# An attention kernel followed by a two-layer block: weights in larger packets, loads reordered, layer work moved forward, decay rows copied directly, the M banks handed out from one tile

## Chip, cores and metric

One core of a Trainium2 chip. The time is device time of the whole program in microseconds. The fast runs of one kernel lie within 1.7% of each other here, most within 1%; ratios below are computed between runs of the same rounds on the same chip. One run of all, at a granted clock of 0.56 against 0.97 to 0.99 in the others, is called slow and left out of the ratios. In the lines of the profile PE is TensorE, PEld its weight loads, DVE VectorE, ACT ScalarE, POOL GpSimd, SP SyncE, and L367 is line 367 of the kernel.

## The reference, cut to what matters

Eight batches of eight heads, 576 positions, head size 64. Causal attention with a decay bias from a running sum of `s`, then a two-layer block over all 4,608 rows.

```python
scores = q @ k.T / sqrt(64)
cum = cumsum(maximum(s, 0))
bias = -(cum[:, None] - cum[None, :])            # clipped at 0, causal mask
attn = softmax(scores + bias) @ v                # x: 4608 x 512
h = x @ w_in                                     # 512 x 2048
out = (h * clip(h + 3, 0, 6) / 6) @ w_out        # 2048 x 512
```

## The kernel before

Heads go in 32 pairs. A pair's q and k are loaded (256-byte rows), cast to f16 on GpSimd, transposed on TensorE; the decay is added through extra rows of kT and qT ("decay rows"). The block runs in nine blocks of 512 rows; a "layer task" is four 512-column matmuls. The kernel uses eight PSUM banks: two called M, three S, two O, one Y. The parts that matter:

```python
cpool / work / psum pools ...
w_in_sb = cpool.tile([128, KC, DFF], F16, tag="c_win")
...
def banks(early):                      # transposes of the first pairs borrow M
    return dict(tag="M", bufs=2) if early else dict(tag="S", bufs=3)
...
def load_w_in(c):                      # four loads, 512 columns each
    nc.gpsimd.dma_start(out=w_in_sb[:, :, c * 512:(c + 1) * 512],
        in_=moe_w_in[:, c * 512:(c + 1) * 512].rearrange("(kc p) f -> p kc f", p=128))
...
def m1(n, f):                          # layer 1
    ph = psum.tile([128, 512], F32, tag="M", bufs=2)      # a new tile for each task
    for kc in range(KC):
        nc.tensor.matmul(out=ph, lhsT=w_in_sb[:, kc, f * 128:(f + 1) * 128],
                         rhs=xT[:, kc, n * 512:(n + 1) * 512], ...)
    trl = work.tile([128, 512], F32, tag="trl", bufs=3)
    nc.scalar.activation(out=trl, in_=ph, func=AF.Relu, bias=bias3[:, 0:1], scale=1.0)
    nc.vector.scalar_tensor_tensor(out=gT[n][:, f, :], in0=trl, scalar=6.0, in1=ph, ...)

def m2(n, t4, part):                   # layer 2; four parts make one output
    if part == 0:
        pouts[n, t4] = psum.tile([128, 512], F32, tag="Y", bufs=1)
...
load_qk(0, nc.sync); load_v(0, nc.scalar); load_qk(1, nc.sync); load_v(1, nc.sync)
load_qk(2, nc.sync); load_v(2, nc.sync)
...                                    # decay rows: SBUF -> DRAM -> rows of each pair
weave(att_of[1], m1_tasks(0))
for n in range(NBLK - 1):
    att = att_of[n + 2] if n + 2 < B else []
    weave(att, merged(m1_tasks(n + 1), m2_tasks(n)))
```

The order of instructions on each engine is the order of this code; the semaphore waits between engines are put in by the framework.

The softmax here doesn't subtract the row's maximum and nothing guards it: scores larger than these inputs give would overflow.

Of the kernel before, what the change touches and what calls it, by code (L numbers as in the profile page):

```python
# [16 lines left out]
def kernel(  # L17
# [23 lines left out]
    GRAN = 10  # L41
    VW = D + 2
# [6 lines left out]
    psum = ctx.enter_context(tc.tile_pool(name="psum", bufs=1, space=bass.MemoryType.PSUM))  # L49

# [68 lines left out]

    def load_qk(p, eng):  # L120
        b, h0 = (2 * p) // H, (2 * p) % H
        t = work.tile([128, NTR, 2, D], F32, tag="qkf", bufs=3, name=f"qkf{p}")
        for i, src in enumerate((q, k)):
            eng.dma_start(
                out=t[:, :, i, :],
                in_=src[b, h0:h0 + 2].rearrange("h s d -> (h s) d").rearrange(
                    "(t p) d -> p t d", p=128
                ),
            )
        qk_f[p] = t  # L130
# [20 lines left out]
    def cast_qk(p):  # L151
        t = work.tile([128, NTR, 2, D], F16, tag="qkh", bufs=2)
        nc.gpsimd.tensor_copy(out=t, in_=qk_f.pop(p))  # L153
        qk_h[p] = t

    def cast_v(p):
        sl = p % NS
        eng = nc.vector if p in (1, 2, 3, 4) else nc.gpsimd
        eng.tensor_copy(out=v_h[:, sl, :, :, 0:D], in_=v_f[:, sl])  # L159

    def banks(early):

        return dict(tag="M", bufs=2) if early else dict(tag="S", bufs=3)

    def transpose_group(p, g):
        t0, t1 = ((0, 5), (5, 9))[g]
        n = (t1 - t0) * 128
        pT = psum.tile([128, 640], F16, **banks(p < 5))
        src = qk_h[p]
        for t in range(t0, t1):  # L170
            nc.tensor.matmul(  # L171
                out=pT[:, (t - t0) * 128:(t - t0 + 1) * 128],
                lhsT=src[:, t, :, :],
                rhs=ident,
                is_transpose=True,
                start=(t == t0),
                stop=(t == t1 - 1),
            )
        sl = p % NS
        c0 = t0 * 128  # L180
        nc.vector.tensor_copy(out=qT[0:64, sl, c0:c0 + n], in_=pT[0:64, 0:n])  # L181
        nc.vector.tensor_copy(out=kT[0:64, sl, c0:c0 + n], in_=pT[64:128, 0:n])  # L182
        if g == 1:
            qk_h.pop(p)
# [95 lines left out]
    def x_transpose(p):  # L280
        b, hp = p // (H // 2), p % (H // 2)
        xs = x_tiles.pop(p)
        pX = psum.tile([128, 640], F16, **banks(p < 3))
# [12 lines left out]
    def load_w_in(c):  # L296
        nc.gpsimd.dma_start(
            out=w_in_sb[:, :, c * 512:(c + 1) * 512],
            in_=moe_w_in[:, c * 512:(c + 1) * 512].rearrange("(kc p) f -> p kc f", p=128),
        )  # L300

    def load_w_out(c):
        nc.gpsimd.dma_start(
            out=w_out_sb[:, c * 4:(c + 1) * 4, :],
            in_=moe_w_out[c * 512:(c + 1) * 512, :].rearrange("(ft p) j -> p ft j", p=128),
        )

# [4 lines left out]
    def m1(n, f):  # L312
        if f == 0:
            gT[n] = work.tile([128, NF, 512], F16, tag="gT", bufs=2, name=f"gT{n}")
        ph = psum.tile([128, 512], F32, tag="M", bufs=2)
        for kc in range(KC):
            nc.tensor.matmul(  # L317
                out=ph,
                lhsT=w_in_sb[:, kc, f * 128:(f + 1) * 128],
# [10 lines left out]
    def m2(n, t4, part):  # L330
        if part == 0:
            pouts[n, t4] = psum.tile([128, 512], F32, tag="Y", bufs=1, name=f"po{n}_{t4}")
# [17 lines left out]


    load_qk(0, nc.sync)
    load_v(0, nc.scalar)
    load_qk(1, nc.sync)
    load_v(1, nc.sync)
    load_qk(2, nc.sync)
    load_v(2, nc.sync)
    mask_rows(0, nc.scalar.copy)
    nc.scalar.activation(out=qaug, in_=c8, func=AF.Copy, scale=-1.0)
    mask_rows(1, nc.scalar.copy)  # L360
    nc.scalar.dma_start(
        out=kaug_dram.rearrange("r (h t) -> h r t", h=NH), in_=kaug
    )
    nc.scalar.dma_start(out=qaug_dram.rearrange("r (h t) -> h (r t)", h=NH), in_=qaug)
    load_aug(0, nc.scalar)
    load_aug(1, nc.scalar)


    def keep_warm(n):
        pw = psum.tile([128, 512], F32, tag="M", bufs=2, name="pw")  # L370
# [5 lines left out]
    weights = {  # L376
        1: [(load_w_in, 0)],
# [128 lines left out]
```

## Time and profile before

| | before |
|---|---|
| median, range | 399.7 us, 396.7 to 401.4 (3 runs) |
| span of the profiled run | 397.3 us |
| TensorE busy | 366.4 us (92%), idle almost only in the first 80 us and at the end |
| DMA engines | full for the first 80 us, half busy to about 280 us, then a tenth or so |

The lines themselves are in the prediction. Read them so: where the row of TensorE is all nines at full clock, only less work on TensorE can save time; where it is not, ask what the chain of waits names.

### The profile page before, as it was taken

What the parts mean: (1) busy time and instruction counts of PE and PEld (TensorE: products, weight loads), DVE (VectorE), ACT (ScalarE), POOL (GpSimd) and SP (SyncE); (2) the same over time, 40 slices, a digit from 0 to 9 for tenths busy, and PEclk for the clock granted to TensorE, in tenths of its full rate; (3) what the DMA queues carried; (4) which work ended last, traced back from release to release, by engine and by line L of the source; (5) the groups of instructions that cost most, each with busy time, mean ns of one, the idle gap of its engine ahead of it and who ended that gap; (6) DMA issues with size and microseconds to landing.
All of it is one profiled execution on the core that took longest, in us unless ns stands there. A gap on an engine that the chain in (4) does not pass through costs nothing.

```text
span 397.3 us, 8194 instructions
## 1 busy us (share of the span) xinstructions
PE 366.4 (92%) x3040; PEld 209.7 (53%) x3040; DVE 227.2 (57%) x417; ACT 210.8 (53%) x406; POOL 140.3 (35%) x333
## 2 busy tenths in 40 slices
PE   7584776899999999999999999999999999999985
PEld 3363443555555555555555555555555544444432
DVE  4574372756666666666666666666665564454511
ACT  6364473755555566666666555555556633443400
POOL 3394825544444444444444444444443200000000
PEclk9999698999999999999999999999999999999999
DMA  9999999955555555554555455455100001010111
GB/s 176 201 213 205 185 208 178 194 108 118 116 118 118 119 117 118 119 117 117 118 118 118 108 126 114 109 126 116 38 28 27 28 26 54 26 53 28 49 58 54
DMA packets 123512, 43.40 MB, mean 109 GB/s; under 512 B 114192, under 2 KB 118672, under 8 KB 123472
## 3 DMA queue, kind: packets, MB, share of 16 engines
q1 hardware_dynamic: 117456, 37.89, 43.9%
q0 software_dynamic: 4224, 4.19, 6.4%
q10 hardware_dynamic: 1792, 0.79, 0.9%
q8 instruction: 24, 0.39, 0.4%
q14 instruction: 16, 0.13, 0.1%
HBM read 37.32 MB, written 9.73 MB: 118 GB/s over the span
## 4 chain that ended last, share of the span: by engine, by line
PE 80%; DMA 10%; POOL 4%; DVE 3%; ACT 2%; issue 1%; SPq 0%; POOLq 0%; ACTq 0%
PE po L335 31%; PE ph L317 29%; PE S L211 8%; DMA qkf<-in_k_dram 7%; PE O L260 6%; PE pT L171 3%; PE pX L285 2%; POOL Pm L224 2%; POOL t L153 1%; DMA kaug_scratch<-kaug 1%; DMA kT<-kaug_scratch 1%; ACT trl L325 1%; ACT Pm L219 1%; DMA s_sb<-in_s_dram 1%; DVE osb L344 1%; DVE gT L326 1%
## 5 line engine op out<-in xcount | busy, mean ns | idle before, releaser
L326 DVE SCALAR_TENSOR_TENSOR gT<-trl,ph 128x512 f16<-128x512 f32 x144 | 98.8, 687 | 114.7 <-ACT trl L325 114.5
L219 ACT ACTIVATE Pm<-S 128x384 f16<-128x384 f32 (+2 forms) x256 | 113.7, 506 | 80.3 <-PE S L211 72.5
L317 PE MATMUL ph<-xT,w_in_sb 128*128 128x512 f16 x576 | 147.4, 381 | 0.0
L335 PE MATMUL po<-w_out_sb,gT 128*128 128x512 f16 x576 | 144.4, 379 | 2.3 <-DVE osb L344 2.3
L325 ACT ACTIVATE trl<-ph,bias 128x512 f32<-128x512 f32 x144 | 99.6, 692 | 82.8 <-PE ph L317 81.0
L224 POOL TENSOR_SCALAR_AFFINE_SELECT Pm<-Pm 128x128 f16<-128x128 f16 (+2 forms) x256 | 78.8, 313 | 154.6 <-ACT Pm L219 144.8
L211 PE MATMUL S<-qT,kT 128*128 128x320 f16 (+4 forms) x448 | 71.4, 265 | 8.0 <-DMA kT<-kaug_scratch 3.0
L335 PEld LDWEIGHTS <-gT 128*128 128x128 f16 x576 | 51.2, 98 | 49.4 <-issue 3.2
L317 PEld LDWEIGHTS <-w_in_sb 128*128 128x128 f16 x576 | 52.2, 98 | 44.5 <-issue 1.1
L211 PEld LDWEIGHTS <-kT 128*128 128x128 f16 x448 | 42.1, 99 | 35.3 <-issue 4.9
L153 POOL CAST t<-qkf 128x1152 f16<-128x1152 f32 x32 | 36.7, 1147 | 21.4 <-DMA qkf<-in_k_dram 21.4
L260 PEld LDWEIGHTS <-Pm 128*128 128x128 f16 x960 | 37.4, 97 | 7.8 <-POOL Pm L224 1.6
L260 PE MATMUL O<-v_h,Pm 128*128 128x65 f16 x960 | 40.8, 193 | 0.5 <-POOL Pm L224 0.5
L171 PE MATMUL pT<-ident,t 128*128 128x128 f16 x288 | 26.8, 222 | 13.5 <-POOL t L153 12.9
L181 DVE COPY qT<-pT 64x640 f16<-64x640 f16 x64 | 28.3, 442 | 17.7 <-PE pT L171 17.6
L171 PEld LDWEIGHTS <-t 128*128 128x128 f16 x288 | 21.1, 99 | 28.1 <-POOL t L153 14.6
L344 DVE TENSOR_SCALAR osb<-po 128x512 f32<-128x512 f32 x36 | 24.8, 690 | 13.8 <-PE po L335 13.2
L182 DVE COPY kT<-pT 64x640 f16<-64x640 f16 x64 | 29.4, 459 | 0.9
L272 DVE TENSOR_TENSOR xs<-O,r 128x640 f16<-128x640 f32 x32 | 26.4, 824 | 1.1
L159 POOL CAST v_h<-v_f 128x640 f16<-128x640 f32 x28 | 20.1, 718 | 0.0
L285 PEld LDWEIGHTS <-xs 128*128 128x128 f16 x160 | 11.8, 99 | 10.9 <-issue 6.2
L293 DVE COPY xT<-pX 128x576 f16<-128x576 f16 x32 | 14.5, 453 | 1.7 <-PE pX L285 1.5
(29 smaller groups left out, 56.6 us busy)
## 6 DMA issues: line engine op xcount, KB each, us to landing
qkf<-in_q_dram SPq DMA_DIRECT2D x32, 288.0 KB
qkf<-in_k_dram SPq DMA_DIRECT2D x32, 288.0 KB
out_dram<-osb SPq DMA_DIRECT2D x36, 256.0 KB
v_f<-in_v_dram SPq DMA_DIRECT2D x62, 128.0 KB
w_in_sb<-in_moe_w_in_dram POOLq DMA_DIRECT2D x4, 512.0 KB, 8.1
w_out_sb<-in_moe_w_out_dram POOLq DMA_DIRECT2D x4, 512.0 KB, 10.1
v_f<-in_v_dram SPq DMA_DIRECT2D x31, 32.0 KB
kT<-kaug_scratch SPq DMA_DIRECT2D x30, 6.8 KB
```

What stands on the lines that cost most here:

```text
L153: nc.gpsimd.tensor_copy(out=t, in_=qk_f.pop(p))
L171: nc.tensor.matmul(out=pT[:, (t - t0) * 128:(t - t0 + 1) * 128], lhsT=src[:, t, :, :], rhs=ident, is_transpose=True, start=(t == t0), stop ...
L182: nc.vector.tensor_copy(out=kT[0:64, sl, c0:c0 + n], in_=pT[64:128, 0:n])
L211: nc.tensor.matmul(out=S[:, c:c + hi - lo], lhsT=kT[:, sl, off + 128 * kt:off + 128 * (kt + 1)], rhs=qT[:, sl, off + lo:off + hi], start=( ...
L219: nc.scalar.activation(out=P[:, p0:p0 + n], in_=S[:, 0:n], func=AF.Exp, scale=0.125, bias=0.0)
L224: nc.gpsimd.affine_select(out=view, in_=view, pattern=pattern, compare_op=ALU.is_ge, fill=0.0, base=0, channel_multiplier=-1,)
L260: nc.tensor.matmul(out=O[:, hh, qt * VW:qt * VW + D + 1], lhsT=P[:, c:c + 128], rhs=v_h[:, sl, hh, kt, 0:D + 1], start=(qt == 0), stop=(qt ...
L317: nc.tensor.matmul(out=ph, lhsT=w_in_sb[:, kc, f * 128:(f + 1) * 128], rhs=xT[:, kc, n * 512:(n + 1) * 512], start=(kc == 0), stop=(kc == ...
L325: nc.scalar.activation(out=trl, in_=ph, func=AF.Relu, bias=bias3[:, 0:1], scale=1.0)
L326: nc.vector.scalar_tensor_tensor(out=gT[n][:, f, :], in0=trl, scalar=6.0, in1=ph, op0=ALU.min, op1=ALU.mult)
L335: nc.tensor.matmul(out=po, lhsT=gT[n][:, f, t4 * 128:(t4 + 1) * 128], rhs=w_out_sb[:, f, :], start=(f == 0), stop=(f == NF - 1),)
L344: nc.vector.tensor_scalar_mul(out=osb, in0=po, scalar1=1.0 / 6.0)
```

## The change

Its intent: weights in 4 and 8 KB packets, loads in order of need, one and a half layers of block 0 beside batch 1, decay rows of pair 0 from SBUF to SBUF. The diff, cut to its core:

```diff
+    Mt = psum.tile([128, 2, 512], F32, tag="M", bufs=1)      # both M banks
+    ring = [0]
+    def bank():
+        ring[0] ^= 1
+        return Mt[:, ring[0], :]
 ...
-        ph = psum.tile([128, 512], F32, tag="M", bufs=2)
+        ph = bank()                       # also early transposes, warm-up
 ...
-                lhsT=w_in_sb[:, kc, f * 128:(f + 1) * 128],
+                lhsT=w_in_t[:, kc, f // 8, f % 8, :],        # every eighth column
 ...
-    def load_w_in(c):                     # 4 loads of 512 columns
+    def load_w_in(h):                     # 2 loads of 1024 columns
+            in_=moe_w_in[:, h * 1024:(h + 1) * 1024]...
+            in_=moe_w_out[h * 1024:(h + 1) * 1024, :].rearrange("(p f) j -> p f j", f=8)[:, f0:f0 + 4, :]
 ...
+            if (n, t4) in ((0, 1), (8, 1), (8, 3)):
+                pouts[n, t4] = bank()
 ...
-    load_v(0, nc.scalar)                  # and v 1, qk 2, v 2 at once on SyncE
+    for hh in range(2):                   # decay rows of pair 0, SBUF to SBUF
+        nc.sync.dma_start(out=kT[64:65, 0, c0:c1], in_=kaug[hh:hh + 1, 0, :])
+        nc.scalar.dma_start(out=qT[67:68, 0, c0:c1], in_=qaug[hh:hh + 1, :])
+    ...
+    load_v(0, nc.sync)                    # then kaug, qaug to DRAM, v 1, qk 2 ...
 ...
+    weights_at = {1: [(load_w_in, 0)], 2: [(load_w_in, 1)]}
+    pairs_at = {0: [3], 1: [4], 2: [], 3: [5], 4: [6], 5: [7, 8]}
 ...
+    first = [(task, 0.0 if f < 4 else 0.7) for f, (task, _) in enumerate(m1_tasks(0))]
+    for c, f in enumerate((0, 2, 5, 8)):  # w_out loads ride on layer tasks
+    weave(att_of[1], first + m2_0[:8])
+    weave(att_of[2], merged(m1_tasks(1), m2_0[8:], 2))
```

A branch for loads by partition is in the new source too, but its switch is 0 and it is never taken.

More of the change, by code (lines that the diff above doesn't have):

```diff
@@ L41 @@
     GRAN = 10
+    PTN = 0
     VW = D + 2
@@ L118, with by_partition @@
     qk_h = {}
+    def by_partition(p):
+        return p < PTN
     def load_qk(p, eng):
         b, h0 = (2 * p) // H, (2 * p) % H
-        t = work.tile([128, NTR, 2, D], F32, tag="qkf", bufs=3, name=f"qkf{p}")
+        t = work.tile([128, NTR * 2 * D], F32, tag="qkf", bufs=3, name=f"qkf{p}")
         for i, src in enumerate((q, k)):
-            eng.dma_start(
-                out=t[:, :, i, :],
-                in_=src[b, h0:h0 + 2].rearrange("h s d -> (h s) d").rearrange(
-                    "(t p) d -> p t d", p=128
-                ),
-            )
+            rows = src[b, h0:h0 + 2].rearrange("h s d -> (h s) d")
+            if by_partition(p):
+                eng.dma_start(
+                    out=t.rearrange("p (i t d) -> p i t d", i=2, d=D)[:, i],
+                    in_=rows.rearrange("(p t) d -> p t d", t=NTR),
+                )
+            else:
+                eng.dma_start(
+                    out=t.rearrange("p (t i d) -> p t i d", i=2, d=D)[:, :, i, :],
+                    in_=rows.rearrange("(t p) d -> p t d", p=128),
+                )
         qk_f[p] = t
@@ L152, in cast_qk @@
         t = work.tile([128, NTR, 2, D], F16, tag="qkh", bufs=2)
-        nc.gpsimd.tensor_copy(out=t, in_=qk_f.pop(p))
+        f = qk_f.pop(p)
+        if by_partition(p):
+            nc.gpsimd.tensor_copy(
+                out=t.rearrange("p t i d -> p i t d"),
+                in_=f.rearrange("p (i t d) -> p i t d", i=2, d=D),
+            )
+        else:
+            nc.gpsimd.tensor_copy(
+                out=t, in_=f.rearrange("p (t i d) -> p t i d", i=2, d=D)
+            )
         qk_h[p] = t
@@ L157, in cast_v, with half_bank, transpose_tile @@
         sl = p % NS
-        eng = nc.vector if p in (1, 2, 3, 4) else nc.gpsimd
-        eng.tensor_copy(out=v_h[:, sl, :, :, 0:D], in_=v_f[:, sl])
-    def banks(early):
-        return dict(tag="M", bufs=2) if early else dict(tag="S", bufs=3)
+        copy = nc.vector.tensor_copy if p in (1, 2, 3, 4) else nc.gpsimd.tensor_copy
+        copy(out=v_h[:, sl, :, :, 0:D], in_=v_f[:, sl])
+    def half_bank(early):
+        if early:
+            return bank().bitcast(F16)[:, 0:640]
+        return psum.tile([128, 640], F16, tag="S", bufs=3, name="pT")
+    def transpose_tile(out, src, first, last):
+        nc.tensor.matmul(
+            out=out, lhsT=src, rhs=ident, is_transpose=True, start=first, stop=last
+        )
     def transpose_group(p, g):
@@ L167, in transpose_group, with transpose_pair @@
         n = (t1 - t0) * 128
-        pT = psum.tile([128, 640], F16, **banks(p < 5))
+        pT = half_bank(p < 5)
         src = qk_h[p]
         for t in range(t0, t1):
-            nc.tensor.matmul(
-                out=pT[:, (t - t0) * 128:(t - t0 + 1) * 128],
-                lhsT=src[:, t, :, :],
-                rhs=ident,
-                is_transpose=True,
-                start=(t == t0),
-                stop=(t == t1 - 1),
+            c = (t - t0) * 128
+            transpose_tile(pT[:, c:c + 128], src[:, t, :, :], t == t0, t == t1 - 1)
+        sl = p % NS
+        c0 = t0 * 128
+        for dst, r0 in ((qT, 0), (kT, 64)):
+            nc.vector.tensor_copy(out=dst[0:64, sl, c0:c0 + n], in_=pT[r0:r0 + 64, 0:n])
+        if g == 1:
+            qk_h.pop(p)
+    def transpose_pair(p):
+        pT = Mt.rearrange("p a b -> p (a b)").bitcast(F16)[:, 0:W2]
+        src = qk_h.pop(p)
+        for t in range(NTR):
+            transpose_tile(
+                pT[:, t * 128:(t + 1) * 128], src[:, t, :, :], t in (0, 8), t in (7, 8)
             )
         sl = p % NS
-        c0 = t0 * 128
-        nc.vector.tensor_copy(out=qT[0:64, sl, c0:c0 + n], in_=pT[0:64, 0:n])
-        nc.vector.tensor_copy(out=kT[0:64, sl, c0:c0 + n], in_=pT[64:128, 0:n])
-        if g == 1:
-            qk_h.pop(p)
+        for dst, r0 in ((qT, 0), (kT, 64)):
+            nc.vector.tensor_copy(
+                out=dst[0:64, sl, 0:W2].rearrange("d (p t) -> d p t", t=NTR),
+                in_=pT[r0:r0 + 64].rearrange("d (t p) -> d p t", p=128),
+            )
     BANKS = [
@@ L282, in x_transpose @@
         xs = x_tiles.pop(p)
-        pX = psum.tile([128, 640], F16, **banks(p < 3))
+        pX = half_bank(p < 3)
         for qt in range(5):
@@ L293, in x_transpose @@
         nc.vector.tensor_copy(out=xT[:, hp, b * SEQ:(b + 1) * SEQ], in_=pX[:, 0:SEQ])
-    def load_w_in(c):
+    def load_w_in(h):
         nc.gpsimd.dma_start(
-            out=w_in_sb[:, :, c * 512:(c + 1) * 512],
-            in_=moe_w_in[:, c * 512:(c + 1) * 512].rearrange("(kc p) f -> p kc f", p=128),
+            out=w_in_sb[:, :, h * 1024:(h + 1) * 1024],
+            in_=moe_w_in[:, h * 1024:(h + 1) * 1024].rearrange("(kc p) f -> p kc f", p=128),
         )
     def load_w_out(c):
+        h, f0 = c // 2, (c % 2) * 4
         nc.gpsimd.dma_start(
             out=w_out_sb[:, c * 4:(c + 1) * 4, :],
-            in_=moe_w_out[c * 512:(c + 1) * 512, :].rearrange("(ft p) j -> p ft j", p=128),
+            in_=moe_w_out[h * 1024:(h + 1) * 1024, :].rearrange("(p f) j -> p f j", f=8)[
+                :, f0:f0 + 4, :
+            ],
         )
+    w_in_t = w_in_sb.rearrange("p k (h m f) -> p k h f m", h=2, f=8)
     gT = {}
@@ L331, in m2 @@
         if part == 0:
-            pouts[n, t4] = psum.tile([128, 512], F32, tag="Y", bufs=1, name=f"po{n}_{t4}")
+            if (n, t4) in ((0, 1), (8, 1), (8, 3)):
+                pouts[n, t4] = bank()
+            else:
+                pouts[n, t4] = psum.tile([128, 512], F32, tag="Y", name=f"po{n}_{t4}")
         po = pouts[n, t4]
@@ L349 @@
     nc.vector.memset(bias3, 3.0)
-    load_qk(0, nc.sync)
-    load_v(0, nc.scalar)
-    load_qk(1, nc.sync)
-    load_v(1, nc.sync)
-    load_qk(2, nc.sync)
-    load_v(2, nc.sync)
-    mask_rows(0, nc.scalar.copy)
-    nc.scalar.activation(out=qaug, in_=c8, func=AF.Copy, scale=-1.0)
-    mask_rows(1, nc.scalar.copy)
-    nc.scalar.dma_start(
-        out=kaug_dram.rearrange("r (h t) -> h r t", h=NH), in_=kaug
-    )
-    nc.scalar.dma_start(out=qaug_dram.rearrange("r (h t) -> h (r t)", h=NH), in_=qaug)
-    load_aug(0, nc.scalar)
-    load_aug(1, nc.scalar)
     def keep_warm(n):
-        pw = psum.tile([128, 512], F32, tag="M", bufs=2, name="pw")
+        pw = bank()
         for i in range(n):
@@ L374, in keep_warm @@
             )
-    weights = {
-        1: [(load_w_in, 0)],
-        2: [(load_w_in, 1), (load_w_in, 2)],
-        3: [(load_w_in, 3)],
-        4: [(load_w_out, 0), (load_w_out, 1)],
-        5: [(load_w_out, 2), (load_w_out, 3)],
-    }
+    load_qk(0, nc.sync)
+    load_qk(1, nc.sync)
+    mask_rows(0, nc.scalar.copy)
+    nc.scalar.activation(out=qaug, in_=c8, func=AF.Copy, scale=-1.0)
+    for hh in range(2):
+        c0, c1 = hh * SEQ, (hh + 1) * SEQ
+        nc.sync.dma_start(out=kT[64:65, 0, c0:c1], in_=kaug[hh:hh + 1, 0, :])
+        nc.scalar.dma_start(out=qT[67:68, 0, c0:c1], in_=qaug[hh:hh + 1, :])
+    for hh in range(2):
+        c0, c1 = hh * SEQ, (hh + 1) * SEQ
+        nc.sync.dma_start(out=kT[65:66, 0, c0:c1], in_=kaug[hh:hh + 1, 1, :])
+        nc.scalar.dma_start(out=kT[66:67, 0, c0:c1], in_=kaug[hh:hh + 1, 2, :])
+    load_v(0, nc.sync)
+    nc.sync.dma_start(
+        out=kaug_dram.rearrange("r (h t) -> h r t", h=NH), in_=kaug
+    )
+    nc.sync.dma_start(out=qaug_dram.rearrange("r (h t) -> h (r t)", h=NH), in_=qaug)
+    mask_rows(1, nc.scalar.copy)
+    load_v(1, nc.sync)
+    load_qk(2, nc.sync)
+    load_aug(1, nc.sync)
+    load_v(2, nc.sync)
+    weights_at = {1: [(load_w_in, 0)], 2: [(load_w_in, 1)]}
+    pairs_at = {0: [3], 1: [4], 2: [], 3: [5], 4: [6], 5: [7, 8]}
     def att_tasks(p):
+        more = p + 1 < NP
         def loads():
@@ L389, in loads @@
                 load_aug(p + 2, nc.sync)
-            if p + 3 < NP:
-                load_qk(p + 3, nc.sync)
-                load_v(p + 3, nc.sync)
-            for load, c in weights.get(p, []):
-                load(c)
-        more = p + 1 < NP
-        tasks = [(loads, 0)]
-        for bi in range(4):
-            tasks.append((lambda bi=bi: scores_bank(2 * p, bi), 400))
-        if p > 0:
-            tasks.append((lambda: attend(2 * p - 1), 1200))
-        if more:
-            tasks.append((lambda: transpose_group(p + 1, 0), 640))
-        for bi in range(4):
-            tasks.append((lambda bi=bi: scores_bank(2 * p + 1, bi), 400))
+            for m in pairs_at.get(p, [p + 3] if p + 3 < NP else []):
+                load_qk(m, nc.sync)
+                load_v(m, nc.sync)
+            if p > 4 and more:
+                cast_qk(p + 1)
         def casts():
@@ L409, in casts, with scores @@
                 cast_v(p + 1)
-            if p + 2 < NP:
+            if p + 2 <= 4:
                 cast_qk(p + 2)
-        tasks.append((casts, 0))
-        if p > 0:
-            tasks.append((lambda: x_transpose(p - 1), 640))
-        if more:
-            tasks.append((lambda: transpose_group(p + 1, 1), 512))
-        tasks.append((lambda: attend(2 * p), 1200))
-        return tasks
+            for load, c in weights_at.get(p, []):
+                load(c)
+        def scores(hd):
+            return [(lambda bi=bi: scores_bank(hd, bi), 400) for bi in range(4)]
+        if not more:
+            tr = []
+        elif by_partition(p + 1):
+            tr = [[(lambda: transpose_pair(p + 1), 1152)], []]
+        else:
+            tr = [[(lambda: transpose_group(p + 1, 0), 640)],
+                  [(lambda: transpose_group(p + 1, 1), 512)]]
+        here = tr if p != 4 else []
+        a = [(loads, 0)] + scores(2 * p)
+        a += here[0] if here else []
+        a += [(lambda: attend(2 * p - 1), 1200)] if p > 0 else []
+        a += scores(2 * p + 1) + [(casts, 0)]
+        a += here[1] if here else []
+        a += [(lambda: x_transpose(p - 1), 640)] if p > 0 else []
+        c = [(lambda: attend(2 * p), 1200)]
+        if p == 4:
+            c += [(lambda: cast_qk(p + 1), 0)] + tr[0] + tr[1]
+        return a, c
+    att_of = [[]]
+    for p in range(NP):
+        a, c = att_tasks(p)
+        att_of[-1] += a
+        if p % 4 == 0 and p > 0:
+            att_of.append([])
+        att_of[-1] += c
+    att_of[-1] += [(lambda: attend(NH - 1), 1200), (lambda: x_transpose(NP - 1), 640)]
     def weave(att, mlp):
         total = float(sum(c for _, c in att)) or 1.0
-        done = 0.0
-        for i, task in enumerate(mlp):
-            while att and done / total < i / len(mlp):
+        whole = float(sum(w for _, w in mlp))
+        done, due = 0.0, 0.0
+        for task, w in mlp:
+            while att and done / total < due / whole:
                 a, c = att.pop(0)
@@ L430, in weave @@
             task()
+            due += w
         for a, c in att:
@@ L434, in m1_tasks, with merged @@
     def m1_tasks(n):
-        return [lambda f=f: m1(n, f) for f in range(NF)]
+        return [(lambda f=f: m1(n, f), 1.0) for f in range(NF)]
     def m2_tasks(n):
-        return [lambda t4=t4, part=part: m2(n, t4, part) for t4 in range(4) for part in range(4)]
-    def merged(a, b):
-        out_ = []
-        for t in range(4):
-            f, g = a[4 * t:4 * t + 4], b[4 * t:4 * t + 4]
-            out_ += [g[0], g[1], f[0], g[2], f[1], g[3], f[2], f[3]]
+        return [
+            (lambda t4=t4, part=part: m2(n, t4, part), 1.0)
+            for t4 in range(4) for part in range(4)
+        ]
+    def merged(a, b, rounds):
+        out_ = []
+        na = len(a) // rounds
+        for t in range(rounds):
+            f, g = a[na * t:na * (t + 1)], b[4 * t:4 * t + 4]
+            if na == 4:
+                out_ += [g[0], g[1], f[0], g[2], f[1], g[3], f[2], f[3]]
+            else:
+                out_ += [g[0], f[0], f[1], g[1], f[2], f[3], g[2], f[4], g[3]] + f[5:]
         return out_
-    keep_warm(22)
+    keep_warm(18)
     cast_qk(0)
-    transpose_group(0, 0)
-    transpose_group(0, 1)
+    if by_partition(0):
+        transpose_pair(0)
+    else:
+        transpose_group(0, 0)
+        transpose_group(0, 1)
     mask_rows(2, nc.vector.tensor_copy)
@@ L454 @@
     cast_qk(1)
-    keep_warm(10)
-    att_all = []
-    cut = []
-    for b in range(B):
-        for p in range(4 * b, 4 * b + 4):
-            att_all += att_tasks(p)
-            if p % 4 == 0:
-                cut.append(len(att_all) - 2)
-    att_all += [(lambda: attend(NH - 1), 1200), (lambda: x_transpose(NP - 1), 640)]
-    cut.append(len(att_all))
-    att_of = [att_all[cut[b]:cut[b + 1]] for b in range(B)]
-    for task, _ in att_all[:cut[1]]:
-        task()
-    weave(att_of[1], m1_tasks(0))
-    for n in range(NBLK - 1):
-        att = att_of[n + 2] if n + 2 < B else []
-        weave(att, merged(m1_tasks(n + 1), m2_tasks(n)))
-    for task in m2_tasks(NBLK - 1):
+    keep_warm(12)
+    for task, _ in att_of[0]:
+        task()
+    first = [(task, 0.0 if f < 4 else 0.7) for f, (task, _) in enumerate(m1_tasks(0))]
+    for c, f in enumerate((0, 2, 5, 8)):
+        task, w = first[f]
+        first[f] = ((lambda task=task, c=c: (task(), load_w_out(c))), w)
+    m2_0 = m2_tasks(0)
+    weave(att_of[1], first + m2_0[:8])
+    weave(att_of[2], merged(m1_tasks(1), m2_0[8:], 2))
+    for n in range(2, NBLK):
+        weave(
+            att_of[n + 1] if n + 1 < B else [], merged(m1_tasks(n), m2_tasks(n - 1), 4)
+        )
+    for task, _ in m2_tasks(NBLK - 1):
         task()
```

## The prediction

> **What bounds the kernel now.** I read the page first: busy shares, the row of slices, the DMA queues.
>
> ```profile
> PE 366.4 (92%) x3040; PEld 209.7 (53%) x3040; DVE 227.2 (57%) x417; ACT 210.8 (53%) x406; POOL 140.3 (35%) x333
> ...
> PE   7584776899999999999999999999999999999985
> ...
> PEclk9999698999999999999999999999999999999999
> DMA  9999999955555555554555455455100001010111
> ...
> q1 hardware_dynamic: 117456, 37.89, 43.9%
> q0 software_dynamic: 4224, 4.19, 6.4%
> ```
>
> A slice is 9.93 us. TensorE is full from the ninth slice to the last two; all its idle time lies in the first 80 us and at the very end. In just those eight slices the DMA row reads 9, afterwards 5. So there are two regimes: a start limited by the arrival of data and a long stretch limited by TensorE. A table of windows cut at the boundaries of the schedule gives the sizes.
>
> ```profile
> 16.07:42.26 26.19, 16.06 (x235) 12.70 (x235) 14.31 (x31) 15.13 (x36) 17.45 (x41) 0.94 1.04 190
> 42.26:82.47 40.21, 32.33 (x314) 20.67 (x315) 24.04 (x46) 25.65 (x52) 21.26 (x50) 0.91 1.01 184
> 82.47:122.62 40.15, 40.15 (x364) 23.86 (x362) 25.28 (x48) 23.51 (x49) 16.95 (x41) 1.00 0.53 110
> ```
>
> Columns: length, then busy us of PE, PEld, DVE, ACT, POOL, then clock, DMA share, GB/s. Row 2 is attention of batch 1 with layer 1 of block 0 (16 tasks of four 512-column matmuls); row 3 is attention of batch 2 with 32 such tasks. Both last 40 us, though row 2 has half the layer work. Row 3 has no idle at all, so nothing there or later can be gained except at the end. Next, the chain that ended last, between 8 and 83 us, in order of time.
>
> ```profile
> 8.12 4.22 DMA kaug_scratch<-kaug
> ...
> 12.41 3.57 DMA kT<-kaug_scratch
> ...
> 29.03 11.91 DMA qkf<-in_k_dram
> ...
> 45.22 16.20 DMA qkf<-in_k_dram
> ...
> 61.54 1.16 POOL t L153
> ```
>
> The first two pieces are the trip of the decay rows through DRAM, before the first scores at 16.07. The other two are k loads of pairs 5 and 7, issued at 29.03 and 45.22 while weights are moving. TensorE's timeline shows what they cost:
>
> ```profile
> 42.26 0.71 PE L171 MATMUL pT<-ident,t 128*128 128x128 f16 x5 [6.91 <-POOL t L153]
> 62.74 0.62 PE L171 MATMUL pT<-ident,t 128*128 128x128 f16 x5 [4.66 <-POOL t L153]
> ```
>
> **What the Trainium skill says.** (1) "DMA: Bandwidth & Descriptors", section "Why small descriptors are slow (HBM only)": every packet carries a fixed overhead. The trace agrees: queue q0 (weights, 2 KB read per packet) takes 0.064 x 397.3 x 16 / 4224 = 96 ns per packet; q1 takes 0.439 x 397.3 x 16 / 117456 = 23.8 ns, or 20.8 ns for its 256-byte packets if its 4,608 output packets of 2 KB also take 96 (estimate). Per byte the small ones cost 1.7 times as much. (2) The same page, "Issuing engines are not separate DMA queues": all queues share the 16 engines and interleave. The 16.2 us landing of pair 7's k beside weights issued by GpSimd agrees. (3) "SBUF — State Buffer", "Door 1: The DMA port swizzle": SBUF has 16-byte lines, and accesses that each go to a new line pay a penalty. The new layer-1 weight loads step 8 f16 elements, exactly 16 bytes. No weight load of the kernel before is strided, so no trace here shows the penalty. (4) "TensorE: Matmul & The Clock Gate", "HAM oscillation — how this bites in real kernels": idle gaps over about 3.4 us drop the clock. Here the slices with the 6.9 and 4.7 us gaps or just after them read 6 and 8, and the five transposes take 0.71 and 0.62 us instead of 0.44.
>
> **The change part by part.**
>
> *Packets.* w_in: two loads of 512 packets (4 KB read) for four of 512 (2 KB); w_out: four of 128 (8 KB) for four of 512. A line through 256 B at 20.8 ns and 2 KB at 96 ns gives 10 ns + 0.042 ns per byte, so 183 ns at 4 KB and 355 at 8 KB (estimates): (1024 x 183 + 512 x 355) / 16 = 23.1 us of all engines, against 4224 x 96 / 16 = 25.4. I take 3 us of DMA time saved, since the bytes stay. GpSimd also issues fewer descriptors: eight issues of 0.76 us become two such and four shorter, some 3 us, spread over the attention of batch 0 and the start of batch 1.
>
> *Decay rows of pair 0.* The chain has 4.2 + 3.6 us here; a direct copy is one landing, which I put at 2 to 3 us, and v of pair 0 no longer shares the engines with q and k of pairs 0 and 1. First scores at 12 to 13 us instead of 16.07. But pair 1 still goes through DRAM, behind v 0, v 1 and qk 2, and the engines are full: total bytes decide when pairs 4 to 7 arrive. I count nothing of this for the end; it becomes waiting further on.
>
> *Order of loads.* A pair (q, k, v; 3,456 packets of 256 B) costs 3456 x 20.8 / 16 = 4.5 us. Pair 5 now waits behind w_in and in front of w_out. Pair 7's k stays behind all weights, because the last w_out issues belong to the ninth of 16 layer-1 tasks. Check with before: 7.67 pairs x 4.5 + 25.4 = 60 plus a start of 2, against 61.5 seen. So pair 7 comes at 61.5 - 3 = 58.5, its transpose at 59.7 instead of 62.74.
>
> *The schedule.* This is the main term. In the old order TensorE had run 7 layer-1 tasks when it stood at pair 7's transpose, and 9 were left; from 62.74 to 82.47 it took 19.7 us, of which 9 x 0.865 = 7.8 us were layer tasks and 11.9 attention of some 2.5 pairs. (In row 3 a pair's attention costs (40.15 - 32 x 0.865) / 4 = 3.1 us, so 7.8: the rest is latency and the cold clock.) In the new order batch 1 carries 24 tasks. By the weights of the weave, the transpose of pair 7 comes after 38% of the attention and 14 tasks; four to five of these run at once while pair 5 is awaited, filling most of the 6.9 us gap. Left are 10 tasks = 8.65 us, and attention between 7.8 and 11.9; I take 9.5. Batch 1 ends at 59.7 + 18.2 = 77.9. Batch 2 has 24 tasks instead of 32: 40.15 - 8 x 0.865 = 33.2, plus 1 for the denser attention, ends at 112.1. Before: 122.62. Gain **10.5 us**. From here both kernels do the same work, TensorE full.
>
> *The end.* Two outputs of block 8 go into the M banks. The three waits
>
> ```profile
> PE po L335 <- DVE osb L344: 2.3, 3, 0.8
> ```
>
> vanish: **2.3 us**. Last eviction and store stay. The fewer early warm-up matmuls run before any data is there: nothing.
>
> *Sum.* 10.5 + 2.3 = 12.8 us; 399.7 - 12.8 = **387 us**.
>
> **Rivals.**
> *A: loads hide it, waits move.* If SyncE's ordered queue delays v or pair 4 (v 0 now stands behind the waits for the decay rows; the cast of pair 4 stands on GpSimd ahead of selects), batch 0 ends later and DMA engines idle meanwhile. For it: 256-byte rates cannot rise, and the DMA row is already 9. Against it: TensorE now has layer tasks in those gaps. Gain then 4 to 7 us: 393 to 396.
> *B: strided weight loads.* If a load goes from 98 ns to some 200, it still hides under a 512-column matmul (0.865 / 4 = 216 ns); only the first after a short matmul shows: perhaps 72 such places x 0.1 = 7 us, leaving 394. If it goes past 216 ns, each extra 50 ns costs 576 x 0.05 = 29 us and the kernel is slower. For it: the skill's line size. Against: PEld is busy 59% in row 3 and is a port of its own, and the stride chosen is just one line.
> *C: no waits left.* If TensorE never waits after the first scores at 12.5, batch 0 takes 18 to 19 us (GpSimd-bound: 9.99 busy of 10 between 20 and 30), batches 1 and 2 each 24 x 0.865 + 4 x 3.1 = 33.3 and some 2 of latency each: end of batch 2 near 101 to 103, a gain of 20 + 2.3: 377 to 379. Against: 58.5 us for pair 7 by bytes alone.
>
> **Range and chances.** Between C in part and A: **380 to 393**. B's bad half I give 5%, A and B's mild half together about 17% of ending within 2% (above 391.7). Faster by over 2% 0.78, within 2% 0.17, slower 0.05. The three runs of before spread over 1.2%, which is in the range too.
>
> **What would show it.** Right if: first scores at 12 to 13 us; the gap before pair 5's transposes under 3 us with four or five layer-1 tasks just ahead of it; pair 7's transpose near 60; no clock below 9 after 20 us; the first matmul of m2 of block 1 near 112; windows from there on as long as before; no waits of po for osb; q0 near 1,700 packets and 5.8% of the shorter span. Wrong if: weight loads of layer 1 stay visible (matmuls of ph spaced over 216 ns in mid-kernel, steady batches over 40.2 us), the gap at pairs 5 to 8 returns at full length, or pair 4's cast waits for its load. The single step I trust least is the split of time between pair 7's landing and the end of batch 1.

## The result, and the profile after

| | before | after |
|---|---|---|
| median, range | 400.6 us, 396.7 to 402.8 (4 runs) | 476.6 us, 474.8 to 478.6 (4 runs) |
| span of the profiled run | 397.3 us | 473.4 us |
| layer-1 matmul waiting for the gT write | not among the waits | 69.8 us, 69 times |
| layer-1 weight load, mean | 98 ns | 145 ns |

The ratio is 1.194, with a 95% interval of 1.182 to 1.205. A ratio is the mean time of one kernel's fast runs over that of the other's in the same rounds, so not quite the ratio of the medians quoted. The kernel became 19% slower where 3% faster was predicted.

The page of the kernel after, the rows that answer to those of before (engines and slices; a slice is now 11.8 us):

```profile
PE 383.1 (81%) x3038; PEld 239.7 (51%) x3038; DVE 229.3 (48%) x417; ACT 213.4 (45%) x406; POOL 138.1 (29%) x331
...
PE   6775665898878888888888888888888877677786
...
PEclk9879599999999999999999999999999999999999
DMA  7899993385444444444444444442000000100011
```

The nines of TensorE have become eights and sevens from the tenth slice to the end. So the loss is not one of the opening, where nearly all of the change acts; it is in each steady batch. A stretch of 40.15 us in mid-kernel, in the table of windows (length, busy us of PE, PEld, DVE, ACT, POOL, clock, DMA share, GB/s):

```profile
200.00:240.15 40.15, 35.47 (x310) 23.28 (x310) 21.92 (x41) 20.27 (x41) 14.79 (x34) 1.00 0.53 116
```

310 matmuls where the steady batch of before had 364, at full clock, with weight loads not busier than before. The list of waits names the partner (engine and line; waited for; total us, times, longest):

```profile
PE Mt L367 <- DVE gT L376: 69.8, 69, 1.5
```

And the chain that ended last, from 44 us on, shows what such a wait is made of:

```profile
44.16 0.89 PE Mt L367 x3
...
45.06 0.70 ACT trl L375
...
45.78 0.70 DVE gT L376
...
46.53 1.55 PE Mt L367 x4
...
48.10 0.69 ACT trl L375
...
48.82 0.70 DVE gT L376
...
49.56 1.88 PE Mt L367 x4
```

Each layer task starts only when ScalarE and VectorE have emptied the bank of the task just before it, 0.70 + 0.70 us and some handing over. With two banks it should have waited for the task before that. In the compiled program of the kernel after, 150 layer-1 matmuls carry a wait on VectorE, in that of before 97. What they wait for differs too: of the 144 layer tasks, the first matmul of 141 waits for the gT write of the task just before in the kernel after, and of none in that of before, where 89 wait for the gT write of the task before that and 55 carry no such wait. Two things could be behind the longer time: the one tile that now holds both banks, or the slower, strided weight loads. That is what the first experiments separate.

### The profile page after: what moved, and what is told of

Its sections match the earlier page's. It is cut to its first block, busy times and chain, and to the rows that moved or that the text cites. A ratio compares the mean times of both kernels' runs of the same rounds, so it can differ in the third digit from the quotient of the medians.

```text
span 473.4 us, 8198 instructions
## 1 busy us (share of the span) xinstructions
PE 383.1 (81%) x3038; PEld 239.7 (51%) x3038; DVE 229.3 (48%) x417; ACT 213.4 (45%) x406; POOL 138.1 (29%) x331
## 4 chain that ended last, share of the span: by engine, by line
PE 57%; DVE 23%; ACT 11%; DMA 5%; issue 2%; POOL 1%; SPq 0%; ACTq 0%; POOLq 0%
PE Mt L367 26%; PE po L389 17%; DVE gT L376 13%; ACT trl L375 10%; PE S L254 5%; DVE xs L315 4%; PE O L303 3%; DVE kT L210 2%; DMA w_in_sb<-in_moe_w_in_dram 2%; DVE qT L210 2%; PE Mt L389 2%; PE pT L328 2%; PE pT L195 2%; DVE r L313 1%; DMA amask<-amask 1%
## 5 line engine op out<-in xcount | busy, mean ns | idle before, releaser
L367 PE MATMUL Mt<-xT,w_in_sb 128*128 128x512 f16 x576 | 152.0, 387 | 72.6 <-DVE gT L376 69.8
L376 DVE SCALAR_TENSOR_TENSOR gT<-trl,Mt 128x512 f16<-128x512 f32 x144 | 98.9, 687 | 201.4 <-ACT trl L375 201.4
L375 ACT ACTIVATE trl<-Mt,bias 128x512 f32<-128x512 f32 x144 | 99.0, 687 | 165.0 <-PE Mt L367 163.0
L367 PEld LDWEIGHTS <-w_in_sb 128*128 128x128 f16 x576 | 80.5, 145 | 114.2 <-issue 85.4
L389 PE MATMUL po<-w_out_sb,gT 128*128 128x512 f16 x528 | 133.2, 379 | 0.0
L254 PE MATMUL S<-qT,kT 128*128 128x320 f16 (+4 forms) x448 | 67.1, 267 | 4.7 <-DMA kT<-kaug_scratch 2.4
L210 DVE COPY qT<-pT 64x640 f16<-64x640 f16 (+1 forms) x54 | 24.0, 445 | 4.8 <-PE pT L195 4.2
L210 DVE COPY kT<-pT 64x640 f16<-64x640 f16 (+1 forms) x54 | 24.8, 459 | 0.7
L195 PE MATMUL pT<-ident,t 128*128 128x128 f16 x243 | 22.7, 221 | 0.0
L336 DVE COPY xT<-pT 128x576 f16<-128x576 f16 x29 | 13.1, 453 | 1.0 <-PE pT L328 0.7
## 6 DMA issues: line engine op xcount, KB each, us to landing
w_in_sb<-in_moe_w_in_dram POOLq DMA_DIRECT2D x2, 1024.0 KB, 10.3
```

The source lines that it names most:

```text
L195: nc.tensor.matmul(out=out, lhsT=src, rhs=ident, is_transpose=True, start=first, stop=last)
L210: nc.vector.tensor_copy(out=dst[0:64, sl, c0:c0 + n], in_=pT[r0:r0 + 64, 0:n])
L254: nc.tensor.matmul(out=S[:, c:c + hi - lo], lhsT=kT[:, sl, off + 128 * kt:off + 128 * (kt + 1)], rhs=qT[:, sl, off + lo:off + hi], start=( ...
L367: nc.tensor.matmul(out=ph, lhsT=w_in_t[:, kc, f // 8, f % 8, :], rhs=xT[:, kc, n * 512:(n + 1) * 512], start=(kc == 0), stop=(kc == KC - 1),)
L389: nc.tensor.matmul(out=po, lhsT=gT[n][:, f, t4 * 128:(t4 + 1) * 128], rhs=w_out_sb[:, f, :], start=(f == 0), stop=(f == NF - 1),)
```

## The experiments

All kernels were correct. Each was timed in three rounds against the kernel before, whose median was 399.4 to 399.8 us in these rounds. The first four ran on one chip, the next four on a second, the last six on a third; differences of a microsecond or two between these groups are less sure than those within one.

### Two tiles for the two M banks

```diff
-    Mt = psum.tile([128, 2, 512], F32, tag="M", bufs=1)
+    Mb = [psum.tile([128, 512], F32, tag=f"M{i}", bufs=1) for i in range(2)]
     def bank():
         ring[0] ^= 1
-        return Mt[:, ring[0], :]
+        return Mb[ring[0]][:, :]
```

> The changed kernel with its two M banks as two tiles of one bank each; nothing else differs. Theory S (one tile for both banks makes each layer-1 task wait for the eviction of the task before it): the 69 waits of the layer-1 matmul on the gT write, 69.8 us, go to near zero, steady batches return to about 40.2 us, and the time is 385 to 393 us. Rival L (the strided weight loads, 145 ns for 98, starve the matmuls): the time stays near 470 us and the waits stay. Rival O (order of loads and schedule): the loss is in the first 110 us and stays.

Measured: 395.7 us median, ratio 0.989 (0.982 to 0.995). One of four runs, the profiled one, was slow (640.9 us at a clock of 0.56) and is left out of the ratio; more on it at the end. Three lines of allocation are worth 476.6 - 395.7 = 81 us. (The edit also blanks a line of the branch that is never taken.) The time is a little above the range that I gave for theory S; the other two theories are out as the cause of the loss. In this compiled program no layer task waits for the gT write of the one just before it; 80 wait for that of the one before that.

### The same fault put into the kernel before

```diff
-        ph = psum.tile([128, 512], F32, tag="M", bufs=2)
+        ph = bank()            # bank() from one [128, 2, 512] tile, as in the change;
                               # also the early transposes and the warm-up
```

> The kernel before with its two M buffers made one tile of two banks, used in turn; weights, loads and schedule as before. Theory S: waits of the layer-1 matmul on the gT write of 60 to 75 us appear, steady batches grow from 40.2 to 48 or more, the time is 460 to 480 us. Rivals L and O: 400 us as before, since neither is in it.

Measured: 469.1 us, ratio 1.171 (1.164 to 1.179). Waits, and a steady stretch of the same length, of this kernel:

```profile
PE Mt L325 <- DVE gT L334: 60.1, 81, 2.0
```

```profile
200.00:240.15 40.15, 35.66 (x316) 20.83 (x315) 22.89 (x43) 20.95 (x41) 15.58 (x36) 1.00 0.48 109
```

One allocation, with nothing else of the change, makes the kernel before 17% slower, with the same wait (142 of 144 tasks in the compiled program) and the same thinning of TensorE, a little less than the batches of 48 us that I expected (46 us, an estimate from 316 matmuls where before has 362 in this stretch). Putting the one tile in costs 469.1 - 399.8 = 69 us, taking it out of the change gives 81 back, more than the whole loss of 77. What makes up the 12 us between the two is not separated.

### Old weights in the two-tile version

```diff
-    w_in: 2 loads of 1024 columns, w_out: 8 KB runs, lhsT=w_in_t[:, kc, f // 8, f % 8, :]
+    w_in: 4 loads of 512 columns,  w_out: 2 KB runs, lhsT=w_in_sb[:, kc, f * 128:(f + 1) * 128]
```

> The two-tile version with the weights of before: packets of 2 KB read, layer-1 weights contiguous, at the same two places of issue. Theory S with the loads hidden: within 1% of the two-tile version, perhaps 2 to 3 us slower from DMA time; weight loads 98 ns again. Rival L: faster than the two-tile version by 5 us or more.

Measured: 396.4 us, ratio 0.991 (0.984 to 0.998), against 395.7: no difference that these runs show. Since the profiled run of the two-tile version is the slow one, this trace shows what two tiles do to the wait and to the steady stretch:

```profile
PE M L364 <- DVE gT L373: 2.1, 5, 0.6
```

```profile
200.00:240.15 40.15, 40.15 (x363) 23.96 (x361) 25.76 (x48) 24.24 (x49) 17.02 (x41) 1.00 0.55 117
```

### New weights alone in the kernel before

> The kernel before with the new weight packets and the strided layer-1 weight loads alone, w_in halves issued in steps 1 and 2. Theory S: 394 to 400 us, weight loads 145 ns hidden below 216 ns. Rival L: 410 us or more, steady batches above 41 us.

Its edit is the reverse of the last one, applied to the kernel before. Measured: 399.8 us, ratio 0.998 (0.990 to 1.005). Weight loads (PEld) and a steady stretch:

```profile
L322 PEld LDWEIGHTS <-w_in_sb x576: 140/144/173, 46.6 to 377.3; 128*128 128x128 f16 x192
```

```profile
200.00:240.15 40.15, 40.15 (x360) 26.23 (x358) 25.36 (x49) 24.02 (x48) 16.88 (x40) 1.00 0.54 117
```

The load with a step of 16 bytes takes 144 ns in place of 98, and TensorE stays full: 144 is below the 216 ns of a 512-column matmul and hides. Rival L is out. The packets did what I had worked out (5.6% of 398.7 us = 22.3 us of all 16 engines for weights, against 25.4) and it moved the time by nothing that shows.

### What is left: 395.7 us where 387 was predicted

The fault aside, the change gave 1.1% in place of 3.2%. Three views of the two-tile version with old weights point to the opening. DMA share and GB/s are the last two columns (a share of 1 or more is read here as full), first of before, then of this version:

```profile
8.00:12.00 4.00, 1.93 (x16) 1.10 (x16) 2.30 (x7) 1.64 (x2) 2.41 (x3) 1.00 1.31 246
12.00:16.00 4.00, 1.08 (x6) 0.29 (x3) 1.23 (x2) 0.00 (x0) 0.55 (x1) 1.00 1.33 235
```

```profile
8.00:12.00 4.00, 2.59 (x18) 1.44 (x19) 3.69 (x8) 1.68 (x2) 0.49 (x1) 1.00 0.40 60
12.00:16.00 4.00, 1.68 (x11) 0.82 (x9) 0.00 (x0) 2.21 (x5) 1.66 (x2) 1.00 0.79 177
```

In its timeline SyncE issues in the order of the program. It is now at the copies of the decay rows from 6.2 to 10.3 us, which wait for ACT and VectorE, and v 0 goes out at 10.4 us, where ACT had sent it at 2.3. For 4 us the engines have almost nothing to move, in a stretch where bytes are the limit. Four kernels test this and two other suspicions.

> The two-tile version (395.7 us) with the opening of before: v of pair 0 on the ACT queue, decay rows of pair 0 through DRAM with the others, SyncE free of waits. In the trace of the two-tile version with old weights the DMA engines were 0.40 busy between 8 and 12 us and 0.79 to 12 to 16, where before had 1.3. Theory D (the new opening holds up SyncE's ordered queue, so all later loads start late): 388 to 392 us, DMA share over 1 from 4 to 16 us, pair 5's cast 4 us or more earlier. Rival V (GpSimd's order behind v 5 alone is to blame): 395 to 397, and first scores 3 us later are lost or hidden.

> The two-tile version with the cast of v 5 put behind the cast and the transposes of pair 5 on GpSimd (there it waited 5.6 to 5.9 us for v 5 while q and k of pair 5 stood ready behind it). Theory V: pair 5's transposes 3 to 5 us earlier and the time 391 to 393. Theory D alone: the wait moves to the next load, 394 to 396.

> The two-tile version with the schedule of before (16 layer tasks beside batch 1, 32 beside batch 2), loads as in the new one. If the new schedule gives what I predicted for it (it moves 8 tasks of 0.865 us into waiting time): slower by 5 to 8 us, 401 to 404 us. If waits of TensorE for loads take that time anyway: within 2 us of 395.7.

> The two-tile version with the decay rows of pair 0 copied from SBUF to SBUF, but issued from ACT, and v 0 from ACT first; SyncE issues its loads without waiting, as in before. Theory D: as good as the old opening or 1 to 3 us better (387 to 391), since first scores are early and no DMA time is lost. If the direct copy itself costs the time: 394 to 397.

Their edits, each to the two-tile version:

```diff
# old opening
-    decay rows of pair 0 SBUF to SBUF; v 0, v 1, qk 2, v 2 on SyncE behind them
+    load_v(0, nc.scalar); v 1, qk 2, v 2 at once on SyncE; kaug, qaug to DRAM and load_aug(0), load_aug(1) on ACT
# cast of v 5 late
-    casts(): cast_v(5) at the end of pair 4's step, before w_out and cast_qk(5)
+    cast_v(5) after cast_qk(5) and its transposes
# old schedule
-    weave(att_of[1], first + m2_0[:8]); weave(att_of[2], merged(m1_tasks(1), m2_0[8:], 2))
+    weave(att_of[1], first);            weave(att_of[2], merged(m1_tasks(1), m2_tasks(0), 4))
     # all tasks of `first` at weight 1.0; output (0, 1) back in bank Y
# rows from ACT
+    v 0 and the SBUF to SBUF copies issued by ACT; SyncE as in the old opening
```

| version | median us | ratio to before (95%) |
|---|---|---|
| two tiles | 395.7 | 0.989 (0.982 to 0.995) |
| + old opening | 392.0 | 0.983 (0.976 to 0.990) |
| + cast of v 5 late | 395.1 | 0.989 (0.982 to 0.997) |
| + old schedule | 396.3 | 0.992 (0.987 to 0.998) |
| + rows from ACT | 393.7 | 0.986 (0.980 to 0.992) |

Theory D holds: with the old opening the engines are at 1.31 and 1.33 again in those two stretches, and 3.7 us come back (the ranges of the fast runs do not overlap: 390.9 to 393.1 against 395.5 to 395.9; the two ran on different chips). With the rows from ACT, where SyncE's queue is free but the direct copy stays, 2.1 us come back; this 393.7 lies in neither range that I expected, and the direct copy issued from ACT is not better than the trip through DRAM. Theory V alone is worth nothing that shows here. And the schedule, my main term, is worth 0.6 us in this company, with ranges that overlap.

The trace with the old opening showed a further wait, in TensorE's timeline:

```profile
37.44 0.39 PE L367 MATMUL M<-xT,w_in_sb 128*128 128x512 f16 x1
42.22 4.25 PE L367 MATMUL M<-xT,w_in_sb 128*128 128x512 f16 x11 [4.39 <-DMA w_in_sb<-in_moe_w_in_dram]
```

The first layer task runs one matmul and then stands 4.4 us for the second half of w_in, which it does not read. In the compiled program the second weight load of the task waits for the second load's queue; in the kernel before, where the operand is contiguous, it waits for the first alone. The version with old weights, whose reads are contiguous, has no such wait either. For this check the kernel before with new weights was also built, not run, with contiguous reads in place of strided ones: the wait for the second load then stands at the ninth task. So it is the strided read that is taken to touch its neighbours' part. Two tiles, one for each half, put the second wait where it belongs, at the ninth task.

> The version with two M tiles and the old opening (392.0), plus w_in in two tiles only. Theory W: the 4.4 us wait goes, but the transposes of pair 5 still stand behind the cast of v 5: 390 to 392, part of the gain appears as a longer wait there.

> Two M tiles, the old opening, the cast of v 5 behind pair 5's, and w_in as two tiles, one for each half. In the version with the old opening the first layer task ran one matmul at 37.4 and then stood 4.4 us until the second half of w_in, which it does not read, had landed. Theory W (one tile for both halves makes the first half wait for the second) with D and V: 386 to 389 us, no such wait. If pair 5's loads then take the time instead: 390 to 392, as with the old opening alone.

> The first version of this call with the schedule of before. With the loads right, what my prediction credited to the schedule should show: 5 to 8 us slower than the new schedule. If the schedule is worth nothing: equal within 2 us.

> The first version of this call with the decay rows of pair 0 copied from SBUF to SBUF from the ACT queue. If an early start of the scores only becomes waiting for later loads, as predicted: equal within 2 us; if it counts: 2 to 3 us faster; in the earlier pair (393.7 against 392.0) it was 1.7 us slower.

```diff
-    w_in_sb = cpool.tile([128, KC, DFF], F16, tag="c_win")
+    w_in_h = [cpool.tile([128, KC, 1024], F16, tag=f"c_win{h}") for h in range(2)]
```

| version (two M tiles, old opening, two w_in tiles, and ...) | median us | ratio to before (95%) |
|---|---|---|
| nothing more | 390.6 | 0.980 (0.973 to 0.986) |
| cast of v 5 late | 393.3 | 0.986 (0.980 to 0.992) |
| cast of v 5 late, old schedule | 393.8 | 0.988 (0.982 to 0.995) |
| cast of v 5 late, rows from ACT in place of the old opening | 393.4 | 0.986 (0.979 to 0.994) |

The wait for w_in is gone; the medians differ by 1.4 us, with ranges that overlap (389.8 to 392.0 against 390.9 to 393.1) and on different chips, so a gain is not shown. Against my expectation, putting the cast of v 5 out of the way cost 2.7 us. GpSimd's timeline says why; first the version without the late cast, then the one with it:

```profile
44.39 0.72 POOL L186 CAST v_h<-v_f 128x640 f16<-128x640 f32 x1 [5.96 <-DMA v_f<-in_v_dram]
45.05 1.10 POOL L349 DMA_DIRECT2D w_out_sb<-in_moe_w_out_dram  x2
```

```profile
38.44 1.10 POOL L349 DMA_DIRECT2D w_out_sb<-in_moe_w_out_dram  x2
...
52.32 0.72 POOL L186 CAST v_h<-v_f 128x640 f16<-128x640 f32 x1 [7.69 <-DMA v_f<-in_v_dram]
54.67 1.15 POOL L178 CAST t<-qkf 128x1152 f16<-128x1152 f32 x1 [1.63 <-DMA qkf<-in_k_dram]
```

The wait for v 5 had been holding back w_out. Without it w_out goes out 6.6 us earlier and shares the engines with v 5 and pair 6, which come 7 to 8 us later though they are needed first. TensorE then stands before pair 6's transposes (this version):

```profile
55.88 0.71 PE L195 MATMUL pT<-ident,t 128*128 128x128 f16 x5 [6.92 <-POOL t L178]
```

That gave the last two kernels: one measures the schedule without this effect, the other keeps the late cast and ties w_out to later tasks.

```diff
-    for c, f in enumerate((0, 2, 5, 8)):
+    for c, f in enumerate((7, 8, 10, 12)):
```

> The version with two M tiles, the old opening and w_in in two tiles (390.6), with the schedule of before. If the schedule fills waiting time there: 394 to 398 us, transposes of pair 7 with fewer layer tasks ahead of them and an idle stretch. If the schedule is worth nothing: 390 to 391.5.

> The version of 393.3 us (cast of v 5 behind pair 5's) with the four w_out loads tied to layer tasks 7, 8, 10 and 12 in place of 0, 2, 5 and 8. If early w_out beside v 5 and pair 6 was the loss: 387 to 390 us, no idle stretch over 4 us before pair 6's transposes. If the moved cast itself loses: stays at 392 to 394.

| version (two M tiles, old opening, two w_in tiles, and ...) | median us | ratio to before (95%) |
|---|---|---|
| old schedule | 394.5 | 0.989 (0.981 to 0.996) |
| cast of v 5 late, w_out late | 387.9 | 0.973 (0.965 to 0.982) |

Here the schedule is worth 394.5 - 390.6 = 3.9 us (ranges 394.1 to 396.1 and 389.8 to 392.0). TensorE's timeline of the old schedule before pair 5's transposes, then of the new one at the same place:

```profile
47.50 1.14 PE L195 MATMUL pT<-ident,t 128*128 128x128 f16 x9 [7.94 <-POOL t L178]
```

```profile
47.35 0.65 PE L195 MATMUL pT<-ident,t 128*128 128x128 f16 x5 [3.06 <-POOL t L178]
```

The transposes start at nearly the same moment, when the data are there; in the new schedule five layer tasks run ahead of them, in the old one a single one. The last version is the fastest of all, 2.7% below the kernel before (the interval takes in 2%, so on record the verdict is unclear). Its four runs spread from 385.9 to 391.5, so against the 390.6 us version (389.8 to 392.0) it is not clear of it; against the version that differs only in where w_out is issued (393.1 to 394.0) it is. Its GpSimd timeline has w_out behind pair 6's cast, and no wait of TensorE over 2.0 us is left between 17 and 130 us:

```profile
47.70 1.15 POOL L178 CAST t<-qkf 128x1152 f16<-128x1152 f32 x1 [2.35 <-DMA qkf<-in_k_dram]
...
49.85 1.10 POOL L349 DMA_DIRECT2D w_out_sb<-in_moe_w_out_dram  x2
```

## Why the prediction was wrong, step by step

**The step that failed.** "Batch 2 ... ends at 112.1. ... From here both kernels do the same work, TensorE full." They do the same work, but not with the same waits. I read the new ring of banks as a new name for the old two buffers and gave it no term in the sum; the prediction mentions the M banks only as a place for two outputs. In its place the runs showed: 69.8 us of waits of a layer task on the eviction of the one before it, 81 us of time, removed by two tiles and reproduced in the kernel before by one. I had named the sign of it ("steady batches over 40.2 us") but hung it on the strided weight loads.

**Rival B**, to which I gave 5% for a slower kernel, has the right verdict and the wrong cause: the strided load is slower, by 46 ns, and hides. Even the mild loss that I estimated for it does not show (0.998).

**Packets.** 23.1 us predicted for the weights, 22.3 measured; right, and worth nothing in time.

**Decay rows.** First scores "at 12 to 13 us": 13.87 after, 12.67 in the two-tile version with old weights. "I count nothing of this for the end": too kind. The copies are free, but the queue in front of which they wait is not; 3.7 us. This was rival A's mechanism, with a smaller size. The two-tile version's 395.7 lies in A's range of 393 to 396, but that is in part luck: it is 8.7 us short of the 387 predicted, and freeing the queue gave back only the 3.7.

**Order of loads.** I put pair 7 at 58.5 us from bytes alone. With old weights and two tiles GpSimd begins its cast at 69.0 us (61.5 in the kernel before): an idle queue early, then w_out beside pairs that are needed sooner. The bytes were right, the assumption that the engines are always fed with what is needed next was not.

**The schedule.** 10.5 us predicted for the whole start, the schedule its main part. Measured for the schedule alone: 0.6, 0.5 and 3.9 us, depending on what else stands in the way; the whole start of the 390.6 us version gave 376.36 - 370.02 = 6.3 us (the first matmul of the last block's second layer, before and there). Moving work into a wait earns only what that wait is long, and another wait may take its place.

**The end.** 2.3 us predicted. From the first matmul of the last block's second layer to the end of the span: 397.3 - 376.36 = 20.9 us before, 388.1 - 370.02 = 18.1 us in the 390.6 us version. Right.

**What stays open.** How much is the clock: an upper estimate of what a low clock costs is the span times one minus the mean granted clock. It gives 10.0 to 11.8 us in the four runs of the kernel after (the clock was 0.51 from 20 to 30 us and 0.50 from 50 to 60) and 6.7 to 8.7 in the fast runs of two tiles: by this estimate some 3 of the 81 us, so nearly all is the wait. For the small differences it weighs more: by the same estimate 1 to 2 us of each of the 3.7, 2.7 and 3.9 us above would be clock, and no run separates that from the waits that go with it. Two tiles with old weights took 394.7 us in a run at 0.987 and 398.7 in one at 0.974. Open is also whether the last version is really better than the one at 390.6.

## What to carry to other kernels

Two buffers are two buffers only if whatever places the waits sees them as two: before trusting a ring inside one tile, look in the compiled program, or in the list of waits, at whom the second user waits for; the same holds for a strided read of one half of a tile while the other is loading. Where bytes limit the start, judge a new order of loads by whether the DMA row stays full and by what shares it, and look for waits that by accident hold back transfers that are not yet needed. A change of many parts should be costed line by line of the diff, the lines that look like renaming included.

## What the Trainium skill lacked or had wrong

- "SBUF — State Buffer", "Door 1: The DMA port swizzle", says that accesses which each go to a new 16-byte line pay a penalty, without a size for weight loads, and in the next sentence counts a stride of 8 bf16 as free. Here a 128-column f16 weight load with just that step, 16 bytes, took 144 ns against 98, and cost nothing that shows beside 512-column matmuls (ratio 0.998).
- "DMA: Bandwidth & Descriptors", "Why small descriptors are slow (HBM only)", works out 27% overhead for 256 bytes from one of its two causes. Per byte, 256-byte packets cost 1.7 times as much here as 2 KB ones (20.8 and 96 ns, the first partly an estimate; the two are on different queues, but q1's own 2 KB output packets took about 90 ns in the last microseconds, an estimate from 0.16 of 16 engines for 58 GB/s); going on to 4 and 8 KB saved only 25.4 - 22.3 = 3.1 us for all weights.
- "TensorE: Matmul & The Clock Gate", "HAM oscillation — how this bites in real kernels", has the clock fall after idle gaps over about 3.4 us; for the falls after shorter idles that the page goes on to report it gives no length. In the kernel after the clock fell to 0.50 at about 47 us and stayed there to 60, where TensorE's gaps were at most 1.5 us, between bursts of 0.9 to 1.9. And one run of the two-tile version had a mean of 0.56 over its whole 639.2 us with TensorE 98% busy; the three other runs of it had 0.98. No page that I found names such a value for a program on one core.
- No page that I found says that waits are placed by tile, so that two banks in one tile lose their double buffering (69.8 us of waits here), or that a strided read of a tile waits for a load of its other half (4.4 us).
